# Weight blocks loaded in pieces, and a lead-in with part of its transposes done by DMA: a transformer layer on one Trainium2 core

## The chip, the core and the metric

The kernel runs on one core of a Trainium2 chip. The core has five engines with queues of their own: TensorE (PE in the profile; its weight loads are listed as PEld), VectorE (DVE), ScalarE (ACT), GpSimd (POOL) and SyncE (SP). Here SP issues all DMAs. The metric is the device time of one execution in microseconds, lower is better.

## The reference

One layer with a norm ahead of each half, on 2048 tokens of width 1024, in bfloat16: softmax attention with 32 heads of 32, then a dense layer of width 3584 with the tanh form of gelu.

```python
def _A_ref(x, wqkv, wo):                      # H = 32, Dh = 32
    qkv = (x @ wqkv).reshape(B, S, 3, H, Dh).transpose(2, 0, 3, 1, 4)
    q, k, v = qkv[0], qkv[1], qkv[2]
    p = softmax(einsum("bhqd,bhkd->bhqk", q, k) * Dh ** -0.5)
    o = einsum("bhqk,bhkd->bhqd", p, v)
    return o.transpose(0, 2, 1, 3).reshape(B, S, D) @ wo

def _B_ref(x, w1, b1, w2, b2):
    return gelu(x @ w1 + b1) @ w2 + b2

h  = x + _A_ref(layernorm(x), wqkv, wo)
h2 = h + _B_ref(layernorm(h), w1, b1, w2, b2)
```

## The kernel before

The program first builds a graph of tasks (`Graph.add`). A task has an engine, one or more instructions, a modelled cost, reads and writes of buffers, and a priority. `Graph.schedule` then plays the engines against these modelled costs and so fixes the order of each engine's queue once and for all; on the chip every engine runs its list in that order, with semaphores between them. For PE, `pick_pe` chooses among the ready tasks: score products (`qk`) first, then products of probabilities and values (`pv`) once enough rounds wait and the tasks in `gate` are done, else the other matrix products (`bg`), of which the one written first in the program is taken. SP takes the ready DMA with the lowest priority number. `assign` gives each DMA one of 24 semaphore lanes.

The 2048 tokens are 16 tiles of 128. The 32 heads are eight groups of four (`g`), and the queries eight blocks of 256 (`qb`). A job is one block with one group: eight rounds of 256 keys. A round is eight score products (L784) into PSUM, two exponentials on ACT (L795, tile `PT`, or `PX` for the extra slots), a pair sum on DVE (L836, tile `PS`), the value products (L821) and the products that form the denominators (L850). PSUM has eight banks: 0 to 5 hold scores, and banks 6 and 7 are handed out one at a time (`slot()`) to every other product and to the jobs' sums.

The lead-in goes tile by tile. `x_tile` loads a tile into one of eight slots of `xrb`; `ln_tiles` normalises two at a time (statistics L598 on DVE, small steps on POOL, the normalised form into one of four slots of `xb`, L613); `tr_tile` transposes it on PE (L619, eight products into one bank) and copies it out into `xnT`, by ACT for tiles 0 to 3 (L626) and by DVE for the others (L628). `proj_half` makes the keys of group 0 for two tiles (L758 copies them to `KT`), and for the first three pairs the queries too. The rounds of the first three jobs (`NLJ = 3`, blocks 0 to 2 of group 0) run as soon as their keys are there; their value products wait in `pending` order until the values of group 0 (`proj_v1`, L740) are ready. `hold` keeps DVE's pair sums of these jobs behind the last key half.

Behind the lead-in, `rest_of_projections(g)` makes the queries and keys (`proj`, L669) and the values (`proj_v1`, `proj_v`, L721) of the other groups, from weights in `Wall` that `rest_w` loads. Queries of a few later blocks go through the staging tile `stg` to memory. Transposed x of the last three quarters is copied to memory too (`xd`, `x_scratch` in the profile), and `late_q` reads it back later. From about 300 us on the jobs of blocks 3 to 7 run beside `wo`, `ln2`, `ffn1` and `ffn2` of earlier blocks. `ln2` transposes by DMA (L575, `hnT`). The weights stream through two rings: `w1r` with four slots of 512 KB (also used for `wo`), filled by `wblock`, and `w2r` with seven slots of 512 KB, filled in `ffn2`. For the last block both rings lie in the space of the keys and values (`b_w1r`, `b_w2r`). All plain matrix products go through `mm` (L546 in four column strips, L549 and L552 in one).

Of the kernel before, what the change touches and what calls it, by code (L numbers as in the profile page):

```python
# [12 lines left out]
P = 128  # L13
# [47 lines left out]
class Graph:  # L61
# [47 lines left out]
    def schedule(self, pick_pe, pool, switch=0.104, dma_rate=280.0, dma_lat=2.1, dma_issue=0.06):  # L109
# [31 lines left out]
        while n < total:  # L141
            if not events:
                raise RuntimeError("schedule: stuck")
            now = heapq.heappop(events)
            while events and events[0] <= now + 1e-9:
                heapq.heappop(events)
            for e in self.ENGS:
                while free[e] <= now + 1e-9:
                    up = upcoming[e]
                    rd = ready[e]  # L150
                    while up and up[0][0] <= now + 1e-9:
                        rd.append(heapq.heappop(up)[2])
                    if not rd:
                        break
                    if e == E.PE:
                        t = pick_pe(rd, now, state, free_banks(now))
                    else:
                        t = min(rd, key=lambda x: (x.prio, num[x]))
                        if up and t.prio > 0:

                            for (rt, _, u) in up[:6]:
                                if u.prio < t.prio and rt < now + 0.6 * t.occ:
                                    t = None
                                    break
                    if t is None:
                        break
                    rd.remove(t)
                    if t.acq is not None:
                        b = min([x for x in free_banks(now) if x in t.acq.banks], key=lambda x: max([y.done for y in pool[x]], default=0.0))
                        t.deps.update(pool[b])  # L170
                        t.acq.n = b
                        pool[b] = t.acq
                    start = now
                    if e == E.PE:
                        if state["mode"] != t.mode:
                            start += switch
                        state["mode"] = t.mode
                    t.order = len(seqs[e])
                    seqs[e].append(t)
                    if e == E.SP:  # L180
                        k = min(range(self.n_lanes), key=lambda i: lanes[i].done if lanes[i] else 0.0)
                        if lanes[k] is not None:
                            t.deps.add(lanes[k])
                            start = max(start, lanes[k].done)
                        lanes[k] = t
                        t.lane = k
                        free[e] = start + dma_issue
                        s0 = max(state["dma"], start + 0.9)
                        state["dma"] = s0 + t.bytes / dma_rate / 1e3
                        t.done = max(state["dma"], s0) + dma_lat - 0.9  # L190
                    else:
                        free[e] = start + t.occ
                        t.done = start + t.occ + t.lat
                    if t.rel is not None:
                        t.rel.rel.append(t)
                        if len(t.rel.rel) == t.rel.nrel:
                            pool[t.rel.n] = t.rel.rel
                        heapq.heappush(events, t.done)
                    heapq.heappush(events, free[e])
                    n += 1  # L200
                    for s in t.succ:
                        s.left -= 1
                        if s.left == 0:
                            release(s)
# [20 lines left out]
    def assign(self, flows, lane_flows):  # L225
# [15 lines left out]
        for e in self.ENGS:  # L241
            c = 0
            for t in self.seqs[e]:
                if e == E.SP:
                    lane_n[t.lane] += 1
                    t.inc = True
                    t.flow = ("L", t.lane)
                    t.value = 16 * lane_n[t.lane]
                else:
                    t.flow = ("E", e)  # L250
                    if t.inc:
                        c += 1
                    t.value = c
# [64 lines left out]
    def emit(self, e, obj):  # L318
        for t in self.seqs[e]:
            for f, v in t.waits:  # L320
                obj.wait_ge(self.sems[f], v)
            ins = None
            for fn in t.fns:
                ins = fn(obj)
            if t.inc:
                ins.then_inc(self.sems[t.flow], 16 if e == E.SP else 1)


def build_kernel(nc, A_x, A_wqkv, A_wo, B_w1, B_b1, B_w2, B_b2, out):
# [188 lines left out]
    def slot(nrel=1):  # L518
        return Slot(gr.buf(), nrel, (6, 7))
# [15 lines left out]
    def drop(t, bank):  # L535
        if isinstance(bank, Slot):
            t.rel = bank

    def mm(bank, lhsT, rhs, start, stop, reads, narrow, cols=(0, 512), after=()):

        c0, c1 = cols
        occ = MM * (c1 - c0) / 512.0 + 0.0026
# [22 lines left out]
    def dma(out_ap, in_ap, nbytes, reads=(), writes=(), prio=0, noncontig=False, after=()):  # L565
        def fn(s):
            if noncontig:
                with nc.allow_non_contiguous_dma(reason="strided gather"):
                    return s.dma_start(out_ap, in_ap)
            return s.dma_start(out_ap, in_ap)  # L570
        return gr.add(E.SP, fn, 0.06, 0.0, reads, writes, prio, nbytes=nbytes, after=after)


    def dma_transpose(out_ap, in_ap, nbytes, reads, writes, prio):
# [75 lines left out]
    def proj(which, g, tc, bank, evac, direct=False):  # L650

        blk, c = divmod(which * D + g * P, 512)
        for dc in range(DC):
            mm(bank, Wall[blk][:, dc, c:c + P], xnT[:, tc, dc, :], dc == 0, dc == DC - 1,
               [B_W[blk][c // P]] + B_xnTt[tc], True)
        if which == 1:
            dst, wr = KT[:, g, 512 * tc:512 * tc + 512], B_KT[8 * g + 2 * tc:8 * g + 2 * tc + 2]
        elif direct:
# [103 lines left out]
    class Att:  # L762
# [8 lines left out]
        def qk(self, job, r, s=None):  # L771


            qb, g = job
            qs = q_slots[qb, g]
            us = [self.unit % self.n_units, (self.unit + 1) % self.n_units]
            self.unit += 2
# [106 lines left out]
    pending = []  # L884

    def attention_round(job, r, lag=1):
        s = att.qk((job.qb, job.g), r)
        pending.append((job, r, s))
        attention_drain(lag)

# [5 lines left out]

    def wblock(R, src_ap, prio=1):
        s = R.next("w1", R.nw1)
        dma(R.w1[:, s, :, :], src_ap.rearrange("(dc p) c -> p dc c", p=P), P * DC * 512, writes=[R.B_w1[s]], prio=prio)
        return s  # L900

    def wo(u, tail=False):
# [84 lines left out]
    def ffn2(u, j, wide=False, W=None, banks=None):  # L987
# [3 lines left out]
        ws = []  # L991
        for q in range(FC // 4):
            s = W.next("w2", W.nw2)
            dma(W.w2[:, s, :, :], B_w2[512 * q:512 * q + 512, c].rearrange("(f p) c -> p f c", p=P),
                P * 4096, writes=[W.B_w2[s]], prio=1)
            ws.append(s)
        for t in range(2):
            bank = banks[t] if banks and banks[t] is not None else slot()
# [25 lines left out]
    for k in range(80):  # L1024
        pe(lambda p: p.matmul(psum[:, 6, 0:256], ident[:, :], b2t[:, 0:256], start=True, stop=True), 0.18 if k < 42 else 0.115,  # L1025
           reads=[B_ident, B_b2t], writes=[B_ps[6]], kind="warm")
    LEAD_ACT = (0, 1, 2, 3)
    NLJ = 3
    last_x = []

    def lead_norm(hc):
        tts = [2 * hc, 2 * hc + 1]
        if hc == 0:
            ln_tiles([0], -3, "dve")
            ln_tiles([1], -2, "dve", 1)
        else:
            ln_tiles(tts, 0, "dve")
        for tt in tts:
            tr_tile(tt, slot(), "act" if tt in LEAD_ACT else "dve")
            if tt + 8 < NT:  # L1040
                last_x.append(x_tile(tt + 8, -4))
        if hc in (3, 5, 7):
            tc = hc // 2
            dma(xd[tc - 1], xnT[:, tc, :, :], P * 8192, reads=B_xnTt[tc], writes=[B_xd[tc - 1]], prio=1)

    lead_rounds = []
    lead_norm(0)
    for hc in range(8):
        ev = "act" if hc == 0 else "dve"
        if hc < NLJ:  # L1050
            proj_half(0, hc, slot(), ev)
        proj_half(1, hc, slot(), ev)
        if hc < 7:
            lead_norm(hc + 1)
        for k, r in [(k, hc) for k in range(min(hc, NLJ))] + ([(hc, r) for r in range(hc + 1)] if hc < NLJ else []):
            n = 8 * k + r
            s = NR + 15 if n == 0 else n - 1 if n < 9 else n
            lead_rounds.append((k, r, att.qk((k, 0), r, s)))
    att.rounds = 8
    hold = [t for t in gr.tasks if t.eng == E.DVE][-1:]  # L1060
    for c in range(4):
        proj_v1(4 * c, 0, 4, slot(), "dve", 0, True)
    gate = gr.tasks[-1]
    for k in range(NLJ):
        job = Job(k, 0, slot(2))
        for _, r, s in [x for x in lead_rounds if x[0] == k]:
            job.pv(r, s)
    pool_banks = {6: [t for t in gr.tasks if t.kind == "warm"][-1:], 7: []}
    lx = last_x[-1:]

    def rest_w(blk, c0, c1):
        load_w(blk, -3, c0, c1, after=lx)

    rest_w(WK, P, 2 * P)
    rest_w(WQ, P, 2 * P)
    rest_w(WV, P, 4 * P)
    rest_w(WK, 2 * P, 3 * P)
    rest_w(WQ, 2 * P, 3 * P)
    rest_w(WK, 3 * P, 4 * P)
# [12 lines left out]
    def rest_of_projections(g):  # L1092
        proj(0, g, 0, slot(), "dve", direct=True)
        for tc in range(4):
            proj(1, g, tc, slot(), "dve")
        if g == 1:
            for c in range(4):
                proj_v1(4 * c, 1, 4, slot(), "dve", 0, True, [gate])
        if g in EXTRA:
            proj(0, g, 1, slot(), "dve")  # L1100
        if g < 7:
# [55 lines left out]
    def ready_rounds(now):  # L1157
# [3 lines left out]
            pv_next[0] += 1  # L1161
        n = pv_next[0]
        waiting = 0
        if gate.done is None or gate.done > now + 1e-9:
            return 0
        while n + waiting < len(pvs) and all(d.done is not None and d.done <= now + 1e-9 for d in pv_exp[n + waiting]):
            waiting += 1
# [110 lines left out]
```

## Time and profile before

| | |
|---|---|
| median of three runs | 1091.22 us (1088.27 to 1091.68) |
| the profiled execution | 1091.97 us, its span 1090.2 us |
| granted TensorE clock | 0.994 |
| busy: PE, ACT, DVE, POOL | 1045.6, 1014.5, 755.9, 43.4 us |
| DMA | 178.03 MB, mean 163 GB/s |
| weight blocks a_w1r of w1, from issue to landing | 98 of 512 KB, 4.4 us |
| weight blocks a_w2r | 105 of 512 KB, 5.7 us |

A line of the costliest groups reads: source line, engine, operation, what is written from what, count, busy time and mean of one in ns, then the idle time of the engine just before and what ended it. The chain goes back from the last instruction to what released each step. A releaser is inferred from semaphores, and "issue" is time in which the engine waited for nothing that the profile shows. The timeline gives the start and the length of merged instructions. Line numbers are those of the kernel before.

### The profile page before, as it was taken

The page shows a single profiled execution, that of the slowest core. Times are in us where ns is not written, and L with a number is a line of the kernel's source. Part 1 is how long each engine was busy: PE and PEld are TensorE (multiplying, and loading weights), DVE is VectorE, ACT ScalarE, POOL GpSimd, SP SyncE. Part 2 cuts the span into 40 slices and gives each one's busy share as a digit, 9 for nine tenths or more (in the row PEclk, how much of TensorE's full clock was granted, in tenths as well). Part 3 has the DMA queues.
Part 4 walks back from the last instruction along what each step waited for, and adds up shares of the span by engine and source line. Part 5 has one row for each costly group of instructions (what it writes and reads, how often), then busy time and mean ns, then how long its engine had stood idle before and what let it go on. Part 6 is the DMA issues. An engine that isn't in the chain of part 4 may idle for free.

```text
span 1090.2 us, 41817 instructions
## 1 busy us (share of the span) xinstructions
PE 1045.6 (96%) x19048; PEld 609.6 (56%) x19107; DVE 755.9 (69%) x1453; ACT 1014.5 (93%) x1116; POOL 43.4 (4%) x110
## 2 busy tenths in 40 slices
PE   8989999998899999999999999999999999999998
PEld 6656555554344664574475457446545754474483
DVE  7886666666576896599489659948974967696401
ACT  4989999999999999999999999999999999999650
POOL 3200000000010001001000100100010000000100
PEclk9999999999999999999999999999999999899999
DMA  7640010008464667665685766567586656987370
GB/s 194 199 123 11 14 41 3 2 3 287 142 167 133 183 180 209 210 189 154 209 251 157 220 215 189 155 217 233 142 239 205 182 179 160 308 236 228 96 246 20
DMA packets 280146, 178.03 MB, mean 163 GB/s; under 512 B 42656, under 2 KB 274976, under 8 KB 279200
## 3 DMA queue, kind: packets, MB, share of 16 engines
q1 hardware_dynamic: 279968, 175.35, 54.1%
q8 instruction: 150, 2.46, 0.9%
q14 instruction: 28, 0.23, 0.1%
HBM read 161.16 MB, written 10.49 MB: 157 GB/s over the span
## 4 chain that ended last, share of the span: by engine, by line
PE 54%; ACT 39%; DVE 5%; issue 1%; DMA 1%; SPq 0%; POOL 0%; POOLq 0%; DVEq 0%
ACT PT L795 35%; PE ps L549 18%; PE ps L546 12%; PE ps L784 8%; PE ps L821 6%; PE ps L552 5%; PE ps L850 3%; ACT PX L795 2%; DVE PS L836 2%; ACT uu L983 2%; DMA xrb<-in_A_x_dram 0%; DVE OD L866 0%; PE ps L1025 0%; SPq L570 0%; DVE OD L873 0%
## 5 line engine op out<-in xcount | busy, mean ns | idle before, releaser
L795 ACT ACTIVATE PT<-ps 128x1024 bf16<-128x1024 f32 x992 | 922.4, 1082 | 14.7 <-PE ps L784 14.3
L836 DVE TENSOR_TENSOR PS<-PT 128x1024 bf16<-128x1024 bf16 x434 | 286.6, 685 | 128.9 <-PE ps L850 68.1
L784 PE MATMUL ps<-QT,KT 32*128 32x256 bf16 x4096 | 205.3, 274 | 10.7 <-ACT PT L795 5.4
L821 PE MATMUL ps<-PT,V 128*32 128x256 bf16 x3968 | 174.4, 274 | 2.8 <-ACT PT L795 2.8
L784 PEld LDWEIGHTS ps<-QT,KT 32*128 32x128 bf16 x4096 | 61.2, 92 | 166.3 <-ACT PT L795 134.8
L850 PE MATMUL ps<-PS,ones 128*32 128x256 bf16 x1792 | 124.6, 275 | 4.8 <-DVE PS L836 4.0
L821 PEld LDWEIGHTS ps<-PT,V 128*32 128x32 bf16 x3968 | 102.1, 97 | 29.4 <-issue 6.8
L549 PE MATMUL ps<-hnT,a_w1r 128*128 128x256 bf16 x949 | 116.5, 274 | 1.1 <-DVE gT L961 0.5
L549 PEld LDWEIGHTS ps<-hnT,a_w1r 128*128 128x128 bf16 x949 | 87.9, 98 | 25.8 <-issue 14.5
L546 PE MATMUL ps<-a_w2r,gT 128*32 128x512 bf16 x1372 | 98.3, 381 | 0.4 <-DVE hch L1007 0.2
L549 PE MATMUL ps<-a_w2r,gT 128*128 128x512 bf16 x382 | 93.8, 380 | 4.2 <-issue 2.9
L546 PE MATMUL ps<-hnT,a_w1r 128*32 128x256 bf16 x2476 | 88.9, 274 | 4.0 <-issue 1.6
L961 DVE TENSOR_TENSOR gT<-ps,b1f 128x512 bf16<-128x512 f32 x98 | 67.2, 686 | 17.5 <-PE ps L546 9.3
L546 PEld LDWEIGHTS ps<-hnT,a_w1r 128*32 128x32 bf16 x2476 | 60.4, 96 | 20.6 <-issue 16.8
L1007 DVE SCALAR_TENSOR_TENSOR hch<-ps,hch 128x512 bf16<-128x512 f32 x32 | 21.9, 685 | 69.9 <-PE ps L552 47.1
L850 PEld LDWEIGHTS ps<-PS,ones 128*32 128x32 bf16 x1792 | 47.0, 96 | 30.7 <-DVE PS L836 14.2
L549 PEld LDWEIGHTS ps<-a_w2r,gT 128*128 128x128 bf16 x413 | 35.2, 98 | 47.4 <-issue 13.4
L549 PE MATMUL ps<-xnT,Wall 128*128 128x512 bf16 (+1 forms) x256 | 53.5, 344 | 4.5 <-DVE rr L876 2.8
L983 ACT ACTIVATE uu<-uu 128x1024 bf16<-128x1024 bf16 x49 | 53.9, 1108 | 0.0
L546 PEld LDWEIGHTS ps<-a_w2r,gT 128*32 128x32 bf16 x1372 | 30.0, 96 | 25.6 <-issue 14.0
L603 POOL CAST mvb<-mv 128x2 bf16<-128x2 f32 (+1 forms) x25 | 4.9, 201 | 987.2 <-DVE mv L600 987.2
L549 PE MATMUL ps<-Wall,xnT 128*128 128x128 bf16 (+1 forms) x443 | 43.9, 247 | 0.0
(89 smaller groups left out, 1007.9 us busy)
## 6 DMA issues: line engine op xcount, KB each, us to landing
a_w2r<-in_B_w_dram SPq DMA_DIRECT2D x105, 512.0 KB, 5.7
a_w1r<-in_B_w_dram SPq DMA_DIRECT2D x98, 512.0 KB, 4.4
a_w1r<-in_A_wo_dram SPq DMA_DIRECT2D x32, 512.0 KB, 4.2
b_w1r<-in_B_w_dram SPq DMA_DIRECT2D x14, 512.0 KB, 6.1
a_w1r<-in_A_wqkv_dram SPq DMA_DIRECT2D x11, 512.0 KB, 5.0
Wall<-in_A_wqkv_dram SPq DMA_DIRECT2D x17, 256.0 KB, 4.7
xrb<-in_A_x_dram SPq DMA_DIRECT2D x16, 256.0 KB, 4.0
hch<-in_A_x_dram SPq DMA_DIRECT2D x16, 256.0 KB, 5.2
```

Of the source, the lines that this page charges most:

```text
L546: fns.append(lambda p, j=j: p.matmul(psum[32 * j:32 * j + 32, bi(bank), c0:c1], lhsT[:, 32 * j:32 * j + 32], rhs, start=start, stop=stop, ...
L549: t.whole = lambda p: p.matmul(psum[:, bi(bank), c0:c1], lhsT, rhs, start=start, stop=stop, skip_group_check=True)
L552: t = pe(lambda p: p.matmul(psum[:, bi(bank), c0:c1], lhsT, rhs, start=start, stop=stop), occ, reads=reads, writes=[bb(bank)], mode="full" ...
L603: pool(lambda g: g.tensor_copy(mvb[:, sl, :], mv_l[:, sl, :]), 0.25, reads=B_mv[sl], writes=B_mvb[sl], prio=prio)
L784: return p.matmul(psum[:, 2 * us[h // 2] + h % 2, 256 * i:256 * i + 256], KT[32 * h:32 * h + 32, g, k0:k0 + P], QT[32 * h:32 * h + 32, qs, :],
L795: act(lambda a, u=u, k=k: a.activation(PTs[s][:, k, :, :], psum[:, 2 * u:2 * u + 2, :], ACT.Exp, bias=0.0, scale=SCALE), 1024, reads=[B_ps ...
L821: fns.append(lambda p, i=i, h=h: p.matmul(psum[32 * h:32 * h + 32, bi(bank), 0:256], V[:, g, 2 * r + i, 32 * h:32 * h + 32], PTs[s][:, h / ...
L836: dve(lambda v: v.tensor_tensor(PS[:, n, :, :], pairs[:, :, 0:256], pairs[:, :, 256:512], ALU.add), c_dve(1024, 2), reads=B_PTs[s], writes ...
L850: fns.append(lambda p, h=h, rhs=rhs, i=i: p.matmul(psum[32 * h:32 * h + 32, bi(bank), 256:512], ones32[:, :], rhs, start=False, stop=last, ...
L961: t = dve(lambda v: v.tensor_tensor(g[:, fc:fc + 2, :], psum[:, bi(bank), :].rearrange("p (f c) -> p f c", f=2), b1f[:, fc:fc + 2].unsquee ...
L983: act(lambda a: a.activation(w, w, ACT.Tanh, bias=0.0, scale=KT2), 1024, reads=[B_uu[i]], writes=[B_uu[i]], prio=-1)
L1007: drop(dve(lambda v, hs=hs, bank=bank, half=half: v.scalar_tensor_tensor(hch[:, hs, c], psum[:, bi(bank), :], half, hch[:, hs, c], ALU.mul ...
```

## The change

- Blocks of the w1 ring are loaded by four DMAs of 32 partitions each, blocks of the w2 ring by two of 64. All pieces of a block count on one semaphore, and the scheduler models an issue for each.
- The transposes of x tiles 10 to 15 are DMA transposes from `xb` to `xnT`, without PE, PSUM bank and DVE copy.
- The first three of the later weight loads wait for x tile 11 instead of the last x tile; the others wait for the last DMA transpose. The copies of transposed x to memory are written after these three.
- `gate` is now two tasks, the last key half of group 0 and the last values of group 0. From the values of group 1 on, every product that begins a sum waits for both (`late`); before, only the values of group 1 waited, for one.
- A staged query projection waits for its staging slot before its first product; before, its copy waited.
- The slots of the first three jobs are made ahead of the lead-in, and `qk` takes the job.

```diff
@@ schedule / assign / emit
-                        free[e] = start + dma_issue
+                        free[e] = start + dma_issue * len(t.fns)
...
-                    lane_n[t.lane] += 1
+                    lane_n[t.lane] += len(t.fns)
...
                 ins = fn(obj)
+                if e == E.SP and fn is not t.fns[-1]:
+                    ins.then_inc(self.sems[t.flow], 16)
@@
+    late = []
+
     def mm(bank, lhsT, rhs, start, stop, reads, narrow, cols=(0, 512), after=()):
+        after = list(after) + (late if start else [])
@@
+    def dma_pieces(piece, nbytes, n, reads=(), writes=(), prio=0):
+        w = P // n
+        fns = [lambda s, a=a: s.dma_start(*piece(slice(a, a + w))) for a in range(0, P, w)]
+        return gr.add(E.SP, fns, 0.06 * n, 0.0, reads, writes, prio, nbytes=nbytes)
@@ proj
+        o = B_stg[cnt["sg"] % NSG]
+        free = o.w + o.r if which == 0 and not direct else []
         for dc in range(DC):
             mm(bank, Wall[blk][:, dc, c:c + P], xnT[:, tc, dc, :], dc == 0, dc == DC - 1,
-               [B_W[blk][c // P]] + B_xnTt[tc], True)
+               [B_W[blk][c // P]] + B_xnTt[tc], True, after=free if dc == 0 else ())
@@ wblock
-        dma(R.w1[:, s, :, :], src_ap.rearrange("(dc p) c -> p dc c", p=P), P * DC * 512, writes=[R.B_w1[s]], prio=prio)
+        src = src_ap.rearrange("(dc p) c -> p dc c", p=P)
+        dma_pieces(lambda q: (R.w1[q, s, :, :], src[q]), P * DC * 512, 4, writes=[R.B_w1[s]], prio=prio)
@@ ffn2
-            dma(W.w2[:, s, :, :], B_w2[512 * q:512 * q + 512, c].rearrange("(f p) c -> p f c", p=P),
-                P * 4096, writes=[W.B_w2[s]], prio=1)
+            src = B_w2[512 * q:512 * q + 512, c].rearrange("(f p) c -> p f c", p=P)
+            dma_pieces(lambda z, s=s, src=src: (W.w2[z, s, :, :], src[z]), P * 4096, 2, writes=[W.B_w2[s]], prio=1)
@@ lead_norm and the lead-in
+    LEAD_PE = 10
...
+    last_t = []
...
-            tr_tile(tt, slot(), "act" if tt in LEAD_ACT else "dve")
+            if tt < LEAD_PE:
+                tr_tile(tt, slot(), "act" if tt in LEAD_ACT else "dve")
+            else:
+                tc, t4 = divmod(tt, 4)
+                last_t[:] = [dma_transpose(xnT[:, tc, :, t4 * P:(t4 + 1) * P], xb[:, tt % NXB, :], P * 2048, [B_xb[tt % NXB]], [B_xnTt[tc][t4]], -4)]
...
-        if hc in (3, 5, 7):
-            tc = hc // 2
-            dma(xd[tc - 1], xnT[:, tc, :, :], P * 8192, reads=B_xnTt[tc], writes=[B_xd[tc - 1]], prio=1)
-
+    lead_jobs = [Job(k, 0, slot(2)) for k in range(NLJ)]
...
         proj_half(1, hc, slot(), ev)
+        lead_k = gr.tasks[-1]
...
-            lead_rounds.append((k, r, att.qk((k, 0), r, s)))
+            lead_rounds.append((k, r, att.qk(lead_jobs[k], r, s)))
...
-    gate = gr.tasks[-1]
+    gate = [lead_k, gr.tasks[-1]]
...
-    lx = last_x[-1:]
+    lx = last_x[3:4]
...
-        load_w(blk, -3, c0, c1, after=lx)
+        load_w(blk, -3, c0, c1, after=list(lx))
...
     rest_w(WV, P, 4 * P)
+    lx = last_t or last_x[-1:]
+    for tc in range(1, 4):
+        dma(xd[tc - 1], xnT[:, tc, :, :], P * 8192, reads=B_xnTt[tc], writes=[B_xd[tc - 1]], prio=1)
@@ rest_of_projections, ready_rounds
+        late[:] = gate
         if g == 1:
             for c in range(4):
-                proj_v1(4 * c, 1, 4, slot(), "dve", 0, True, [gate])
+                proj_v1(4 * c, 1, 4, slot(), "dve", 0, True)
...
-        if gate.done is None or gate.done > now + 1e-9:
+        if any(x.done is None or x.done > now + 1e-9 for x in gate):
             return 0
```

## The prediction

> **What bounds the kernel now.** I read the page first: busy time, the chain, the costliest groups.
>
> ```profile
> PE 1045.6 (96%) x19048; PEld 609.6 (56%) x19107; DVE 755.9 (69%) x1453; ACT 1014.5 (93%) x1116; POOL 43.4 (4%) x110
> PE 54%; ACT 39%; DVE 5%; issue 1%; DMA 1%; SPq 0%; POOL 0%; POOLq 0%; DVEq 0%
> L795 ACT ACTIVATE PT<-ps 128x1024 bf16<-128x1024 f32 x992 | 922.4, 1082 | 14.7 <-PE ps L784 14.3
> ```
>
> TensorE (PE) and ScalarE (ACT) are both nearly full, and the chain changes between them. ACT has a fixed list of exponentials, and they wait for the score products (L784) for only 14.3 us in all. So an idle microsecond of ACT between the first exponentials and the last moves the end by a microsecond. The table by stage shows where such idle time lies (columns: length, busy time of PE, weight loads, VectorE (DVE), ACT, GpSimd, then clock, DMA share, GB/s).
>
> ```profile
> 23.00:72.70 49.70, 44.41 (x810) 29.74 (x810) 44.91 (x92) 49.70 (x54) 7.29 (x16) 1.00 0.46 146
> 72.70:76.50 3.80, 3.37 (x22) 1.43 (x24) 3.55 (x11) 0.01 (x1) 0.00 (x0) 1.00 1.04 235
> 76.50:1022.00 945.50, 914.80 (x17625) 524.47 (x17674) 679.23 (x1289) 937.44 (x1017) 22.23 (x56) 0.99 0.56 166
> 1022.00:1090.00 68.00, 64.51 (x425) 39.79 (x428) 10.76 (x22) 19.36 (x36) 3.45 (x8) 0.99 0.37 123
> ```
>
> From 23 us on ACT is full but for a hole of 3.8 us at 72.7 and 8.1 us (945.5 less 937.4) spread over the long middle. Before 23 us it waits for tiles 0 to 3, which the change leaves alone; after 1022 us a tail of 68 us follows that starts when attention ends. The timeline shows what made the hole.
>
> ```profile
> 48.59 0.99 DVE L613 TENSOR_SCALAR xb<-xrb,mvr,rden 128x1024 bf16<-128x1024 bf16 x2
> 50.83 0.69 DVE L628 COPY xnT<-ps 128x1024 bf16<-128x1024 bf16 x1 [0.27 <-PE ps L619]
> 53.09 0.42 DVE L758 CAST KT<-ps 128x256 bf16<-128x256 f32 x1 [1.57 <-PE ps L549]
> 63.70 6.67 DVE L836 TENSOR_TENSOR PS<-PX 128x1024 bf16<-128x1024 bf16 x11
> 72.90 1.41 PEld L549 LDWEIGHTS ps<-xnT,Wall 128*128 128x128 bf16 x8 [2.25 <-DVE OD L873]
> 75.11 0.65 DVE L669 CAST KT<-ps 128x512 bf16<-128x512 f32 x1
> 76.51 8.36 ACT L795 ACTIVATE PT<-ps 128x1024 bf16<-128x1024 f32 x9 [3.80 <-PE ps L784]
> ```
>
> ACT starves because the keys of head group 1 for its third quarter reach KT only at 75.11. Their projection needs PSUM bank 6 or 7, and both are held by lead-in attention jobs that wait for DVE's pair sums (L836). Those may not start before the last key half of the lead-in (53.09) and run without a break to 72. DVE is the engine in arrears: 44.9 of 49.7 us.
>
> In the middle I looked for PE gaps that wait for nothing shown ("issue" in the chain), by name and length.
>
> ```profile
> 432.75 0.32 PE ps L784 x5
> 433.08 1.23 issue
> 434.31 0.31 PE ps L784 x3
> 815.83 1.49 issue
> ```
>
> Both cut a set of eight score products in two, where no semaphore can be the cause. The windows of 6 us around them have DMA queues at 318 and 343 GB/s. Six such gaps of over 0.4 us between 300 and 1000 us (1.23, 0.52, 0.60, 0.45, 1.49, 0.41) make 4.7 us. The page counts 150 packets, 2.46 MB, on an instruction queue that shares the DMA engines: I read the gaps as PE running dry of instructions while weights stream.
>
> **The change part by part.** *Transposes of tiles 10 to 15.* Gone are 48 PE transposes (L619, 0.62 us a tile, 3.7 us) and six L628 copies of 0.68 us, 4.1 us of DVE. Added are six DMA transposes. The same shape runs in the middle, with these rows (ns of issue, min/median/max, and us to landing):
>
> ```profile
> L575 SPq DMA_TRANSPOSE hnT<-a_xb x14: 1239/1294/3207, 307.9 to 933.1; - x14
> DMA to landing us min/median/max: 2.7/3.7/6.5
> a_w1r<-in_B_w_dram SPq DMA_DIRECT2D x98, 512.0 KB, 4.4
> a_w2r<-in_B_w_dram SPq DMA_DIRECT2D x105, 512.0 KB, 5.7
> ```
>
> Take tile 15, the last. Now its normalised form is ready at 49.58 and its transpose at 51.52: 1.94 us. By DMA it is 1.24 (the issue of tile 14's) plus 3.7, 4.9 us; at worst 1.24 plus 6.5, 7.7. Four earlier copies are gone from DVE by then, so it starts 2.7 us earlier. The last key half thus moves from 53.1 to 53.4, at worst 56.2. ACT needs it at its 22nd lead-in round: the 2nd starts at 22.91, each takes 1.83, so at 59.5. The lateness is covered by 3.3 us or more; without that cover it would cost ACT one for one. PE stands in order: behind a key half that waits for a transpose stand the score products of rounds already due, with about one round (1.83 us) in hand. DVE's normalising of tiles 14 and 15 must wait until DMA has read tiles 10 and 11 (four xb slots): issued after 36.5, landed by 44.3 at worst, needed at about 46. Nothing.
>
> *Banks and gates.* Six takings of a bank go, and for 3 us more (4.9 less 1.94) PE waits for transposes with nothing urgent. A key projection of group 1 costs 8 products of 0.22, 1.7 us, and a copy of 0.69; the second and third need only tiles 4 to 11. Nothing of group 1's keys is gated, while V for later groups is. I expect three quarters of the keys before the lead-in jobs take the banks: 24 + 6 rounds, which feed ACT to 22.91 + 29 x 1.83 = 76. The fourth follows on the first free bank (before: 72.9, now about 71), its copy 2.2 us later, in time. The hole closes: 3.8 us, bounds 0 (projections still behind the jobs) and 3.8 (nothing more to fill there); I take 3.8. The V projections that now wait for both gates are due after 95 us; PE had 5.3 us idle in this stage to make them up.
>
> *Weights, copies, staging.* Three loads (1.31 MB) pass ahead of x tiles 12 to 15: at the 295 to 345 GB/s of the rows from 30 to 40 us that is up to 4.4 us for tile 14, which landed near 27 and is read near 38. The other loads now go out behind the last transpose, near 51, not at 27 and 68; group 2 uses them after 95. The three copies of transposed x (1 MB each) are read back at 258. The staging wait moves from the copy to the first product; its three writes stand at 93, 123 and 139 us with two slots, so it is over each time. Behind the DMA transposes on SP stand only these. Nothing for each.
>
> *Pieces.* 155 w1-ring blocks get 3 issues more, 112 w2-ring blocks one: 577 x 0.367 us is 212 us of SP, which only issues. A w1 block's last piece leaves 1.1 us later. Its ring has four slots and a block's 16 products take at least 1.8 us, 2.2 with scores between: three blocks, 6.6 us, against 4.4 of landing leave 2.2, now 1.1. The Q loads, stores and transposes behind it on SP lose the same 1.1 us and have whole jobs of 14.6 us (8 x 1.83) in hand. Nothing, while pieces move as fast as blocks do. In return the instruction queue may get through sooner. The gaps are worth 0 to 4.7 us; the trace can't tell, and I take the middle, 2.3. The Trainium skill (DMA: Bandwidth & Descriptors, "Queues, rings and completion order") says that a DMA engine changes between queues only at the end of a packet; if a block's share is one packet, all 4.7 could go, and the sum would be 1082.7. No run so far shows how a block is cut into packets.
>
> The sum against the profiled execution: 1091.97 - 3.8 - 2.3 = 1085.9 us. It lies 0.75 above the median of the runs (1091.22), so I forecast 1085.1. What this kernel's measurement can tell from no change is about 0.3%, 3.3 us.
>
> **The rivals.** *A: little is left.* The gaps stay and the hole closes in part, since the written order is remade everywhere and its 8.1 us of small ACT waits may fall otherwise. For it: the hole alone is hardly above 3.3 us. Against: both parts act in it. 1087.4 to 1091, mostly no change.
>
> *B: pieces are slow, and the weights become the bound.* A piece covers 32 or 64 of 128 partitions. If it gets half of the path, it gets half of the best 5 us row (346 GB/s at 550 to 555), 173. One block of 256 tokens repeats every 95.6 us (first w1 products at 548.2 and 643.8) and loads 32 weight blocks, 16.8 MB; with the 203 GB/s of 600 to 700 us, 2.6 MB are other traffic, 7.5 us at full rate. At 173 weights take 97.1: 104.6 us for 95.6, 9 us late each time, 54 over six. DMA bounds the whole stage from 191 GB/s down (16.8 MB in 88.1 us); above it only bursts, such as 540 to 575 us with 247 GB/s, make PE wait. Price 0 to 54, taken at half: 1091.2 - 3.8 + 27 = 1114. For: PE stands in order, and this load is near the limit. Against: every DMA in the trace covers all 128 partitions, so nothing shows the halving. The Trainium skill (SBUF — State Buffer, "Door 1: The DMA port swizzle") states it: 32 or 64 neighbouring partitions reach half of the ports, 189 and 196 GB/s against 328. That is just at the rate named above, so by the skill the lower half of the price would hold: 1087 to 1114.
>
> *C: DMA transposes come late.* Beyond the 3.3 us in hand, or with PE blocked ahead of due scores, ACT idles at 45 to 60 us: 2 to 6 us, with the hole still closed or not 1090 to 1097. Against: 6.5 us was the worst landing among weights, and this stage has 0.02 DMA share at 45 to 50.
>
> **How the numbers follow.** Forecast 0.42, A 0.20, B 0.30, C 0.08. A quarter of A lies beyond 3.3 us: faster 0.47, same 0.15, slower 0.38. The low end takes the whole 4.7 (1082.7) less 1.7 for scatter (the runs span 3.4): 1081. The high end goes into B until about 0.15 is left above: 1112. The forecast's own range is 1081 to 1088.
>
> **What would show it.** ACT without a hole at 72 to 77, and KT of group 1's third quarter copied before 62. Six L628 copies instead of twelve, and six more L575 transposes that land in 2.7 to 6.5 us. "Issue" gaps in the chain under half of 4.7 us. For B: w1 and w2 landings well over 5.5 and 6.8 us, burst rows under 250 GB/s, PE waiting for DMA at L546 and L549. The forecast is wrong if the hole stays, if landing grows by over 2 us, or if ACT's small waits in the middle exceed 8 us.

## The result, and the profile after

The changed kernel takes 1123.35 us (median of 6 runs, 1119.39 to 1124.93) against 1091.44 for the kernel before on the same chip: ratio 1.0284, 95% interval 1.0251 to 1.0317. It is 32 us slower, where I had forecast 6 us faster. The profiled execution took 1122.76 us with a span of 1121.0.

The page of the kernel after, first the chain's shares and the group of the exponentials, then the line of the DMA queue and the two kinds of weight pieces (count, size, median us to landing). L809 is before's L795, and L798 its L784.

```profile
PE 57%; ACT 25%; DVE 6%; DMA 5%; SPq 3%; issue 3%; POOL 1%; POOLq 0%; DVEq 0%
L809 ACT ACTIVATE PT<-ps 128x1024 bf16<-128x1024 f32 x992 | 924.2, 1072 | 45.1 <-PE ps L798 43.9
q1 hardware_dynamic: 295536, 176.96, 65.4%
a_w2r<-in_B_w_dram SPq DMA_DIRECT2D x210, 256.0 KB, 6.3
a_w1r<-in_B_w_dram SPq DMA_DIRECT2D x392, 128.0 KB, 3.0
```

ScalarE's idle time ahead of the exponentials grew from 14.7 to 45.1 us. That is 30.4 us, and the span grew by 30.8: the whole loss passes through this one wait. The DMA queue shows where it comes from. It moved 1.61 MB more than before (the six transposes by DMA), but the time of its packets rose from 54.1% to 65.4% of 16 engines' span. And half a w2 block lands in 6.3 us where the whole block took 5.7.

The table by stage puts most of the loss into the long middle (columns as in the prediction). First the kernel after, then two stages of the kernel before.

```profile
23.00:72.70 49.70, 44.99 (x814) 27.64 (x816) 39.59 (x84) 49.70 (x56) 7.29 (x16) 1.00 0.57 161
72.70:76.50 3.80, 2.38 (x118) 1.67 (x106) 3.40 (x7) 3.80 (x5) 0.00 (x0) 1.00 1.21 313
76.50:100.00 23.50, 22.00 (x621) 16.41 (x626) 14.02 (x27) 18.80 (x21) 0.00 (x0) 0.93 0.33 79
300.00:1000.00 700.00, 660.56 (x12470) 377.35 (x12499) 511.95 (x982) 671.46 (x725) 22.31 (x56) 0.99 0.78 188
```

```profile
76.50:100.00 23.50, 23.08 (x627) 17.10 (x630) 13.16 (x24) 23.27 (x26) 0.00 (x0) 1.00 0.26 63
300.00:1000.00 700.00, 679.83 (x13007) 392.26 (x13039) 532.91 (x1023) 693.97 (x754) 22.23 (x56) 1.00 0.67 197
```

Between 300 and 1000 us ScalarE is now idle for 28.5 us (before 6.0), with the DMA engines busier (0.78 against 0.67) and moving less (188 against 197 GB/s). The same table also shows the lead-in: no hole at 72.7 to 76.5, but 4.7 us lost behind it, at 76.5 to 100 (before 0.2).

The chain of the kernel after names the late transfers, and the waits of PE's weight loads name them again.

```profile
431.73 9.62 DMA a_w2r<-in_B_w_dram
...
831.27 8.89 DMA a_w2r<-in_B_w_dram
...
992.96 6.41 DMA a_w1r<-in_B_w_dram
```

```profile
PEld ps L554 <- DMA a_w2r<-in_B_w_dram: 6.7, 8, 1.3
PEld ps L554 <- DMA hnT<-a_xb: 5.3, 1, 5.3
PEld ps L551 <- DMA a_w1r<-in_B_w_dram: 4.5, 2, 2.4
```

The chain runs through single weight pieces for 6 to 10 us. In the profile of the kernel before, PE's weight loads wait for no weight block, and no weight transfer stands on the chain between 300 and 1000 us. The transpose into hnT is late for another reason: its input is written by 946.9 us, but SP issues it only at 957.7, behind pieces that go out almost without a break, each taking 0.45 us (w1) or 0.62 us (w2) of SP. It then lands 7.2 us later.

### The profile page after: what moved, and what is told of

The parts are those of the page before. It is cut to its first block, busy times and chain, and to the rows that moved or that the text cites. A ratio compares the mean times of both kernels' runs of the same rounds, so it can differ in the third digit from the quotient of the medians.

```text
span 1121.0 us, 42575 instructions
## 1 busy us (share of the span) xinstructions
PE 1052.0 (94%) x19139; PEld 608.7 (54%) x19197; DVE 751.9 (67%) x1447; ACT 1017.9 (91%) x1116; POOL 43.5 (4%) x110
## 3 DMA queue, kind: packets, MB, share of 16 engines
q1 hardware_dynamic: 295536, 176.96, 65.4%
## 4 chain that ended last, share of the span: by engine, by line
PE 57%; ACT 25%; DVE 6%; DMA 5%; SPq 3%; issue 3%; POOL 1%; POOLq 0%; DVEq 0%
ACT PT L809 22%; PE ps L554 19%; PE ps L551 14%; PE ps L798 9%; PE ps L835 6%; PE ps L557 5%; PE ps L864 4%; DMA a_w2r<-in_B_w_dram 3%; SPq L582 3%; DVE PS L850 2%; ACT PX L809 2%; DMA xq<-x_scratch 1%; DVE st L610 1%; DMA a_w1r<-in_B_w_dram 1%; DVE OD L880 1%
## 5 line engine op out<-in xcount | busy, mean ns | idle before, releaser
L809 ACT ACTIVATE PT<-ps 128x1024 bf16<-128x1024 f32 x992 | 924.2, 1072 | 45.1 <-PE ps L798 43.9
L798 PE MATMUL ps<-QT,KT 32*128 32x256 bf16 x4096 | 205.7, 275 | 11.5 <-ACT PT L809 6.8
L798 PEld LDWEIGHTS ps<-QT,KT 32*128 32x128 bf16 x4096 | 61.1, 92 | 166.8 <-ACT PT L809 126.1
L864 PE MATMUL ps<-PS,ones 128*32 128x256 bf16 x1792 | 124.5, 276 | 4.2 <-DVE PS L850 3.6
L554 PEld LDWEIGHTS ps<-hnT,a_w1r 128*128 128x128 bf16 x949 | 88.2, 98 | 30.8 <-issue 13.4
L551 PE MATMUL ps<-hnT,a_w1r 128*32 128x256 bf16 x2476 | 91.3, 279 | 8.8 <-DMA a_w1r<-in_B_w_dram 4.1
L864 PEld LDWEIGHTS ps<-PS,ones 128*32 128x32 bf16 x1792 | 47.2, 97 | 29.9 <-DVE PS L850 11.9
L880 DVE STREAM_TRANSPOSE OD<-ps 128x256 f32<-128x256 f32 x64 | 28.6, 447 | 22.2 <-PE ps L864 14.1
```

The source lines that it names most:

```text
L551: fns.append(lambda p, j=j: p.matmul(psum[32 * j:32 * j + 32, bi(bank), c0:c1], lhsT[:, 32 * j:32 * j + 32], rhs, start=start, stop=stop, ...
L554: t.whole = lambda p: p.matmul(psum[:, bi(bank), c0:c1], lhsT, rhs, start=start, stop=stop, skip_group_check=True)
L798: return p.matmul(psum[:, 2 * us[h // 2] + h % 2, 256 * i:256 * i + 256], KT[32 * h:32 * h + 32, g, k0:k0 + P], QT[32 * h:32 * h + 32, qs, :],
L809: act(lambda a, u=u, k=k: a.activation(PTs[s][:, k, :, :], psum[:, 2 * u:2 * u + 2, :], ACT.Exp, bias=0.0, scale=SCALE), 1024, reads=[B_ps ...
L864: fns.append(lambda p, h=h, rhs=rhs, i=i: p.matmul(psum[32 * h:32 * h + 32, bi(bank), 256:512], ones32[:, :], rhs, start=False, stop=last, ...
L880: t = dve(lambda v: v.transpose(OD[:, o, 1, :], psum[:, bi(bank), 256:512]), 0.36, reads=[self.B_O, self.B_D], writes=B_D, prio=-1)
```

## Experiments: the weight pieces

Three theories stood against each other. T1: a piece over 32 or 64 neighbouring partitions moves slower, and the weights become the bound (rival B). T2: the number of DMAs that SP issues costs the time. T3: the new lead-in and the order planned anew from it cost the time.

**The pieces alone.** The kernel before, with the change's pieces and nothing else:

```
-        dma(R.w1[:, s, :, :], src_ap.rearrange(...), P * DC * 512, ...)
+        dma_pieces(lambda q: (R.w1[q, s, :, :], src[q]), P * DC * 512, 4, ...)
...
+            dma_pieces(lambda z, s=s, src=src: (W.w2[z, s, :, :], src[z]), P * 4096, 2, ...)
```

> The kernel before, with the weight blocks in pieces as in the change (w1 blocks in 4 pieces of 32 partitions, w2 blocks in 2 of 64) and nothing else: the instructions of TensorE, VectorE, ScalarE and GpSimd stand in the same order as before. T1 (a piece that covers 32 or 64 neighbouring partitions moves slower, so the weights become the bound): the whole loss is here, 1116 to 1126 us, ScalarE's waits for the score products 40 to 50 us instead of 14.3, burst windows under 250 GB/s. T2 (the number of DMAs that SP issues costs the time): the same 1116 to 1126 us, but SP busy with issuing ahead of the late pieces, whichever partitions they cover; the run with pieces by chunk tells the two apart. T3 (the new lead-in and the order that is planned anew after it cost the time): 1088 to 1094 us, as before.

1121.53 us against 1091.07: ratio 1.0290 (1.0269 to 1.0310). T3 is out.

**The lead-in alone.** The kernel after with every weight block whole (`dma_pieces(..., 1, ...)`):

> The kernel after, with every weight block loaded whole again; the lead-in and the order of the instructions on TensorE, VectorE, ScalarE and GpSimd are those of after. T1 and T2: the lead-in alone costs little or gains, 1086 to 1094 us; the hole of ScalarE at 77 to 80 us tells how much of the predicted 3.8 us comes. If the hole is there as in the kernel after, 1089 to 1093; if not, 1086 to 1088. T3: 1115 to 1125 us, as after.

1091.12 us: ratio 0.9997 (0.9979 to 1.0014). The loss lies in the pieces alone, and the lead-in is worth nothing that the interval shows.

**As many pieces, cut the other way.** The kernel before with pieces by rows of the weight matrix, so that each covers 128 partitions (shown against the run with the pieces alone):

```
-        dma_pieces(lambda q: (R.w1[q, s, :, :], src[q]), P * DC * 512, 4, ...)
+        dma_pieces(lambda q: (R.w1[:, s, q, :], src[:, q]), P * DC * 512, 4, DC, ...)
...
-            dma_pieces(lambda z, s=s, src=src: (W.w2[z, s, :, :], src[z]), P * 4096, 2, ...)
+            dma_pieces(lambda z, s=s, src=src: (W.w2[:, s, z, :], src[:, z]), P * 4096, 2, 4, ...)
```

> The kernel before, with the weight blocks in as many pieces of the same size as in the change, but cut by the rows of the weight matrix (w1: 4 pieces of two of the eight chunks; w2: 2 pieces of two of the four chunks), so that each piece covers all 128 partitions. T1 (coverage of partitions): 1088 to 1096 us, burst windows over 300 GB/s again. T2 (the number of issues): 1116 to 1126 us, the same as with pieces by partition. T3: as before, 1088 to 1094 us. If smaller pieces let the queue of instructions through sooner, as I predicted, PE's gaps named issue between 300 and 1000 us shrink here from 4.7 us to 0 to 2.4 and the time is 1086 to 1089.

1092.26 us: ratio 1.0024 (1.0007 to 1.0042). The pages of the two, first the pieces by partition and then those by rows:

```profile
q1 hardware_dynamic: 289200, 175.38, 64.2%
a_w2r<-in_B_w_dram SPq DMA_DIRECT2D x210, 256.0 KB, 6.2
a_w1r<-in_B_w_dram SPq DMA_DIRECT2D x392, 128.0 KB, 3.0
```

```profile
q1 hardware_dynamic: 289200, 175.38, 55.3%
a_w2r<-in_B_w_dram SPq DMA_DIRECT2D x210, 256.0 KB, 4.3
a_w1r<-in_B_w_dram SPq DMA_DIRECT2D x392, 128.0 KB, 2.6
```

Packets, bytes and the number of DMAs are the same to the last digit; only the partitions that one DMA reaches, and with them the rows that it reads, differ. The packets take 64.2% of the time in one and 55.3% in the other, and the runs differ by 29 us. T2 is out, but for the 0.24% (2.6 us) by which the second is slower than before.

**The loads by themselves.** Eight forms of 14 weight blocks, one form after the other, in a single execution:

> Only loads, no layer: 14 weight blocks of 512 KB (7.34 MB) in each of eight forms, one form after the other, with a wait for all landings between; nothing else of the computation is done. Forms in order: w1 whole; w1 in 4 pieces of 32 neighbouring partitions; w1 in 4 pieces of two chunks over all partitions; w1 in 4 pieces of 32 partitions, lower and upper half in turn; w2 whole; w2 in 2 pieces of 64 partitions; w2 in 2 pieces of two chunks; w1 in 4 pieces of every fourth partition. T1: about 21 to 25 us (295 to 346 GB/s) for the whole, the by-chunk and the every-fourth forms; 31 to 42 us (173 to 240 GB/s) for the forms of 32 or 64 neighbouring partitions; with lower and upper half in turn between the two, 22 to 42, by whether two pieces in flight share the ports. T2: all forms of four pieces alike (56 issues) and slower than whole, whatever the partitions; two pieces between.

The windows from the first issue of a form to that of the next (length, clock, DMA share, GB/s), in the order of the text above:

```profile
0.73:28.04 27.31, 0.00 (x0) 1.00 1.09 269
28.04:62.72 34.68, 0.00 (x0) 1.00 1.10 212
62.72:94.09 31.37, 0.00 (x0) 1.00 0.84 234
94.09:125.81 31.72, 0.00 (x0) 1.00 1.03 232
125.81:149.42 23.61, 0.00 (x0) 1.00 0.98 311
149.42:183.84 34.42, 0.00 (x0) 1.00 1.03 214
183.84:209.32 25.48, 0.00 (x0) 1.00 0.90 288
209.32:248.51 39.19, 0.00 (x0) 1.00 0.70 187
```

The clean pair is w2 in two pieces: 34.42 us for 64 neighbours, 25.48 by rows, with 28 issues each. In the steady part of each form 64 neighbours get 229 GB/s, pieces by rows 339 and whole blocks 350. For w1 my expectation by T1 was wrong in three of the five forms: whole blocks take 27.31 us and not at most 25, and the pieces by rows and of every fourth partition take over 31 us, as all forms of 56 pieces do. In these two SP sets the pace: 0.469 us a piece by rows, 0.614 us a piece of every fourth partition (56 x 0.614 = 34 us), some 0.05 us between two pieces, and the DMA share stays at 0.84 and 0.70. With 32 neighbours the DMA engines themselves are full (1.10), and a piece lands in 5.2 us at the median, not in 2.7 or 2.9. So both theories hold in this test, each where its resource is full. In the layer the pieces by rows, with all their issues, cost 2.6 us, and T2's part is at most that.

In the form with 64 neighbours lower and upper half take turns, a piece starts every 0.87 us and lands after 9.9 us at the median, so some eleven are in flight (an estimate from these two figures). Pieces of both halves are thus under way together, and the rate is 229 GB/s all the same: what one DMA does not reach, the next one does not make up for.

The Trainium skill (SBUF — State Buffer, "Door 1: The DMA port swizzle") gives a reason: 32 or 64 neighbouring partitions reach 8 of 16 ports, with 189 and 196 GB/s against 328 for all 128, each at 1 MiB. The runs agree in kind: 227 and 229 GB/s against 290 (whole w1 blocks) and 350 (whole w2 blocks). The measured rates of the half are 17 to 20% above the skill's figures.

The runs by themselves do not show that the limit lies in SBUF. In every form a partition and its row of the matrix go together, so a limit on the side of the memory is a rival that none of them separates. That blocks with rows of 512 B and of 1 KB, at 290 and 350 GB/s when whole, come down to the same 227 and 229 GB/s speaks for the receiving side.

**Which of the two.** The kernel before with w1 pieces only, and with w2 pieces only:

> The kernel before with the w1-ring blocks alone in 4 pieces of 32 neighbouring partitions; w2-ring blocks whole. In the loads measured by themselves these pieces ran at 227 GB/s where whole w1 blocks ran at 290, w2 pieces of 64 at 229 where whole w2 blocks ran at 350. If a block's own slowdown sets its share of the 30 us, w1 (155 blocks, 81 MB) loses less than w2 (112 blocks, 59 MB): 155 x 0.50 us = 78 us of extra transfer against 112 x 0.79 us = 88 us; I expect 1097 to 1107. If only the total rate in the bursts matters and either kind by itself still fits, 1090 to 1096.

> The kernel before with the w2-ring blocks alone in 2 pieces of 64 neighbouring partitions; w1-ring blocks whole. T1 (a piece over neighbouring partitions reaches half of the way into SBUF): 1100 to 1112 us, the larger half of the 30 us, since the waits of the kernel after end mostly with w2 loads. If the two kinds only hurt together: 1090 to 1096.

w1 alone: 1101.86 us, ratio 1.0085 (1.0058 to 1.0112). w2 alone: 1117.18 us, ratio 1.0209 (1.0172 to 1.0246), above what I expected. They add up: 0.85% and 2.09% make 2.94%, against 2.90% for both. But w2 costs 2.5 times as much as w1, where I had worked out 88 to 78 from the transfers. That w2's slowdown by itself is larger (229 for 350 against 227 for 290) is not enough. The two traces say more. On the chain from 300 to 1000 us, gaps of PE that wait for nothing shown ("issue", of 0.4 us and more) make 14.9 us with the w2 pieces and 4.1 us with the w1 pieces, where the kernel before has 4.7. That is most of the 13.5 us by which the two differ (2.09 less 0.85%), each sum from one profiled execution. Why w2 pieces make more of these gaps stays open.

**Every second partition.** Two w2 pieces of 64 partitions each, as in the run above, but interleaved:

```
-        fns = [... s.dma_start(*piece(slice(a, a + w))) for a in range(0, P, w)]
+        fns = [... s.dma_start(*piece(slice(a, P, n))) for a in range(n)]
```

> As the kernel with the w2-ring blocks alone in 2 pieces, of 64 partitions each and of the same size, but each piece takes every second partition instead of 64 neighbours. If which partitions a piece reaches is what counts (T1): as before, 1088 to 1094 us, landings of w2 pieces near 4.3 us. If a DMA over fewer partitions is slower whichever they are: as with 64 neighbours, 1100 to 1112, landings near 6.2 us.

1094.32 us against 1092.61: ratio 1.0025 (1.0007 to 1.0043), 0.3 us above what T1 allowed. The pages, first with 64 neighbours and then with every second partition:

```profile
q1 hardware_dynamic: 281760, 175.35, 60.2%
a_w2r<-in_B_w_dram SPq DMA_DIRECT2D x210, 256.0 KB, 6.3
```

```profile
q1 hardware_dynamic: 281760, 175.35, 53.9%
a_w2r<-in_B_w_dram SPq DMA_DIRECT2D x210, 256.0 KB, 4.6
```

The number of partitions is the same and the time is not: it is which partitions a DMA reaches, or which rows it reads with them, that counts. This is as the rule of the Trainium skill (SBUF — State Buffer, "Door 1: The DMA port swizzle") has it, by which every second partition reaches all 16 ports.

## Experiments: where the lead-in's gain went

The hole at 72.7 to 76.5 us closed and nothing was gained that the interval shows. In its place stand waits behind it: the kernel after with whole blocks loses 3.2 us between 72.7 and 100 us, the kernel before 4.0 (3.8 in the hole and 0.2).

```profile
76.50:100.00 23.50, 22.07 (x658) 16.39 (x663) 15.16 (x30) 20.30 (x23) 0.00 (x0) 1.00 0.36 83
```

The timeline of the kernel after with whole blocks, just behind:

```profile
75.01 0.39 PE L864 MATMUL ps<-PX,ones 128*32 128x256 bf16 x6
77.06 0.10 PEld L864 LDWEIGHTS ps<-PX,ones 128*32 128x32 bf16 x2 [1.94 <-issue]
...
78.62 3.77 ACT L809 ACTIVATE PT<-ps 128x1024 bf16<-128x1024 f32 x4 [1.58 <-PE ps L798]
```

PE stops in the middle of a set of eight products and waits for nothing that is shown, while ten Wall loads of 256 KB stream from 70.35 to 82 us (313 GB/s, DMA share 1.21 at 74 to 76). In the changed kernel itself the same gap was 2.76 us and ScalarE's wait 3.82. Theory L1: PE runs dry of instructions in the burst. L2: the gap belongs to the order of PE's work.

**The ten loads spread, after and before.** One load behind each of the first ten rounds of group 1's attention, in the kernel after with whole blocks, and in the kernel before:

```
-    rest_w(WK + 1, 0, P)
...
+    spread = [(WK + 1, 0, P), (WQ + 1, 0, P), (WV + 1, 0, 256)]
...
                 attention_round(job, r)
+                if spread and g == 1:
+                    qk = [t for t in gr.tasks if t.kind == "qk"][-1]
+                    blk, c0, c1 = spread.pop(0)
+                    load_w(blk, -3, c0, c1, after=[qk])
```

> The kernel after with whole weight blocks, and its last ten Wall loads (256 KB each, used from head group 3 on) one by one behind the first ten rounds of group 1's attention instead of in one burst from 70 to 82 us; the order on TensorE, VectorE, ScalarE and GpSimd is unchanged. Theory L1: PE runs dry of instructions while the burst streams (a gap of 1.7 to 2.8 us at 75 to 78 us inside a set of eight products, DMA share 1.2), and that gap eats the lead-in's gain: without the burst the gap is gone, ScalarE loses under 1.5 us between 72 and 100 us, and the time is 1086.5 to 1089.5. Rival L2: the gap belongs to the order of the products or to waits that the trace does not show: it stays, 1089.5 to 1092.5.

> The kernel before with the same ten Wall loads spread over the first ten rounds of group 1's attention instead of in one burst from 68 to 79 us; the order on TensorE, VectorE, ScalarE and GpSimd is unchanged. If the hole of 3.8 us at 72.7 to 76.5 us is made by PSUM banks and pair sums, as I predicted, it stays: 1090 to 1092.5 us. If the burst made it (PE starved of instructions), the hole shrinks to under 1.5 us: 1087 to 1089.5.

After: 1090.45 us, ratio 0.9997 (0.9977 to 1.0018). This decides nothing: the loads still ran from 71.06 to 83.5 us, and a gap of 1.05 us was left. Before: 1090.11 us, ratio 0.9999 (0.9983 to 1.0015). There the DMA share at 72.7 to 76.5 us fell from 1.04 to 0.41 and the hole did not shrink (5.46 us). So the hole of the kernel before is not made by the burst, as predicted.

**The ten loads later.** As above, from the second job on (`and qb > 0`):

> The kernel after with whole weight blocks, and its last ten Wall loads one by one behind the rounds of group 1's second and third attention jobs, from about 91 us on, so that no load streams between 70 and 90 us (the kernel that spread them over the first ten rounds still moved 249 GB/s at 72.7 to 76.5 us and kept a PE gap of 1.05 us). The order on the engines is the same up to about 95 us and differs in places behind that. L1 (PE starved of instructions by the burst): no gap above 0.5 us inside a set of products at 75 to 78 us, ScalarE loses under 1.5 us between 72 and 92 us, 1086.5 to 1089.5 us. L2 (the order of PE's work there): ScalarE still loses 2.5 to 3.5 us between 72 and 92 us in several waits for score products, 1089.5 to 1092.5 us.

1089.59 us against 1091.24: ratio 0.9980 (0.9968 to 0.9992). The timeline at the same place:

```profile
74.64 0.73 PE L864 MATMUL ps<-PX,ones 128*32 128x256 bf16 x8
...
81.09 3.77 ACT L809 ACTIVATE PT<-ps 128x1024 bf16<-128x1024 f32 x4 [0.67 <-PE ps L835]
...
88.37 7.44 ACT L809 ACTIVATE PT<-ps 128x1024 bf16<-128x1024 f32 x8 [1.28 <-PE ps L798]
```

The eight products run through, and ScalarE has no hole from 63.6 to 80.4 us. PE's order up to there is the same as with the burst, so the burst made the gap. The packets of the instruction queue in the traces (q8 on the page, 16 KB each) fit L1: the one that starts at 72.72 us here starts at 74.72 with the burst, and in both PE goes on with the last two of the eight products 1.4 us after the packet's end (73.68 and 75.62).

ScalarE still loses 2.24 us at 72 to 92 (1.5 was L1's limit), in three waits. The first six loads left at 78.5 us and not at 91 as I had meant, so the three waits fall among loads again, and the run does not tell L1 from L2 in what is left. The time lies 0.1 us above the range that I gave for L1, at the lower edge of L2's. This kernel, 0.2% or 2.2 us under the kernel before, has the lowest ratio of all that ran, though its interval overlaps that of the kernel with the burst: that the gap ate the lead-in's gain is not shown by the times.

**Tiles 10 to 15 on PE again.** The kernel after with whole blocks and `LEAD_PE = 16`:

> The kernel after with whole weight blocks and with tiles 10 to 15 transposed by PE again; the gates, the staging wait and the later weights and copies stay as in the change, and the order is planned anew. If the DMA transposes are what relieves VectorE and closes the hole at 72.7 to 76.5 us, that hole is back (2 to 4 us) and the time is 1090 to 1095 us, up to 4 us over the kernel with whole blocks and DMA transposes (1091.1). If the gates close it and PE's 3.7 us of transposes find room, 1089 to 1092 us with ScalarE full at 72.7 to 76.5.

1090.96 us, ratio 0.9999 (0.9985 to 1.0012). ScalarE's timeline:

```profile
64.00 7.65 ACT L809 ACTIVATE PT<-ps 128x1024 bf16<-128x1024 f32 x8
78.22 32.45 ACT L809 ACTIVATE PT<-ps 128x1024 bf16<-128x1024 f32 x35 [6.57 <-PE ps L798]
```

The hole is back, so it is the DMA transposes that close it, and the gates alone do not. In time this kernel can't be told from the one with DMA transposes and the burst (1090.96 and 1091.12 us), though in the profiles its hole of 6.57 us is larger than the waits of 3.2 us there. Where the difference is made up is not shown.

## Why the prediction was wrong, and where it was right

**The transposes: right.** Issue 1.24 us was 1.42, landing 3.7 was 3.4 (3.1 to 4.1); six copies of transposed x are left on VectorE. The last key half was due at 53.4, at worst 56.2, and was copied at 55.17. ScalarE stayed full from 23 to 72.7 us, so the cover held and rival C did not come.

**Banks and gates: right in the mechanism, nothing left in the sum.** The copies of group 1's keys stand at 43.96, 46.12, 48.28 and 60.40 in the kernel after, all ahead of the 62 that I named for the third, and the hole closed. The term of 3.8 us came to 0.3 us (ratio 0.9997, by its interval anything from a gain of 2.3 to a loss of 1.5), and to 2.2 with the ten loads out of the way. What I left out is that ScalarE then waits behind the hole.

**Weights, copies, staging: wrong.** I put nothing, because all data come in time. They do. What I did not price is the traffic itself: I had the late loads leave near 51 us, but only four did; ten were held on SP until 70.0 us (before until 68.0). They fill blocks of `Wall` whose space the extra slots `PX` of the lead-in's exponentials share, so they wait for the last products that read those slots (in the profile 14.9 us of SP for L864). The burst then fell on PE work that ScalarE was waiting for.

**Pieces: the step that failed.** "Nothing, while pieces move as fast as blocks do." They do not: 227 and 229 GB/s measured by themselves, where whole blocks get 290 and 350, and this alone costs 30 of the 32 us. I had the rival with the right mechanism and the right signs, gave it 0.30, and held against it that every DMA in the trace covers all 128 partitions. That is no evidence against it: such a trace cannot show what a part of the partitions gets. Of its price, 0 to 54 us taken at 27, 30 came; that the two are close is luck, since none of it came as I had worked it out. At 227 to 229 GB/s, well above the 191 from which DMA would bound the whole stage, my sum gave nothing but bursts, and I named bursts without pricing them. A sum over the windows of 5 us of the kernel before from 300 to 1050, of what each moved above 229 GB/s, gives 77 us of transfer that would be late if no ring held a reserve. That is the bound from above that the price of late weights needed; the 30 us are two fifths of it. The issues were too small in my sum as well, 0.367 us each against 0.45 and 0.62 measured; pieces by rows, with as many issues of 0.47 us, bound what this cost at 2.6 us.

**Gaps of instructions: wrong sign.** I took 2.3 of the 4.7 us as gained. On the chain from 300 to 1000 us such gaps of 0.4 us and more make 12.6 us in the kernel after and 14.1 with the pieces alone. With pieces by rows they make 0.9, and there the time is not lower but 2.6 us higher. Each sum is from one profiled execution. The reading itself, that PE runs dry of instructions, was right by the traces: all 23 gaps in these sums of the kernel before, the kernel after and the pieces alone end 1.3 to 1.7 us after the end of a packet of the instruction queue, a distance that only 6% of the time from 300 to 1000 us has. So slow pieces hold up instructions as well as weights: by these sums 8 to 9 of the 30 us (12.6 and 14.1 less 4.7). That went into neither rival.

**The range.** It reached 1112 and the result is 1123. The upper end was cut inside rival B, where the price had no row behind it.

## What to carry to other kernels

A DMA cut into pieces by partitions is another transfer, not the same one in smaller parts: cut by rows of the matrix, or take every second partition, so that each piece reaches all 128 partitions or an even share of them. No form of pieces was faster here than whole blocks, so cut only for a reason that a run has shown. A DMA that others slow down can be one that loads instructions: look for gaps that wait for nothing shown before calling all of a loss late data. Where a kernel loads weights in bursts, ask of a slower transfer what the bursts cost and not only whether the mean rate still fits. When a trace shows only one form of an operation, its silence on other forms counts for neither side.

## What the runs showed of the hardware

A piece of every fourth partition takes SP 0.614 us to issue, one of 32 neighbours or of two chunks over all partitions 0.45 to 0.47, at the same 128 KB. For many small pieces the time to issue is a limit of its own: 128 KB in 0.614 us is 213 GB/s, and with the time between two pieces 200 were measured.

Around a PE gap of some 2 us (1.97 and 2.19 us in the two that follow) the granted clock fell in some runs and not in others. The table by stage of the kernel with transposes on PE and of the kernel before with spread loads:

```profile
72.70:76.50 3.80, 3.80 (x10) 1.33 (x9) 2.34 (x7) 0.00 (x0) 0.00 (x0) 0.50 0.92 206
```

```profile
72.70:76.50 3.80, 3.80 (x12) 1.43 (x11) 2.98 (x9) 0.00 (x0) 0.00 (x0) 0.57 0.41 89
```

The clock is the third figure from the end: 0.50 and 0.57, where the profile of the kernel before has 1.00 after a gap of the same 2.19 us as in the second. The key projection that ScalarE waits for then takes longer, and the hole is 6.57 and 5.46 us in place of 3.80. The Trainium skill (TensorE: Matmul & The Clock Gate, "What's actually happening") gives half speed for the throttled state, and 0.50 agrees. It has the clock fall after an idle window of about 3.4 us; the gaps here are shorter, and the clock fell all the same. What tells the runs apart that kept it is open.
